# Decode attention with a gated MLP on one core: V as the moving operand of PV, in groups of four pairs, and output rows split over two PSUM rows

## The chip, the cores and the metric

The kernel runs on one core of one Trainium2 chip. Times are device microseconds of one execution. Before the change three runs took 196.67 to 197.09 us, with a median of 196.91.

The core's engines work from separate instruction streams and meet through semaphores: TensorE (PE: matrix multiply into PSUM; its weight loads, PEld, overlap its matmuls), VectorE (DVE), ScalarE (ACT), GpSimd (POOL) and SyncE (SP), which here issues the large transfers. All transfers run on the same 16 DMA engines.

## The reference

One token x (512 values) goes through two branches, and a gate mixes them. The attention branch has 32 heads, each with its own keys and values in a cache of 4096 positions of 128 values:

```python
g = sigmoid((x * gate_w).sum(-1, keepdims=True))
q = (x @ wq)                              # 32 heads x 128
scores = einsum("bhqd,bhkd->bhqk", q, k) * (128 ** -0.5)
p = softmax(scores)
o = einsum("bhqk,bhkd->bhqd", p, v)
a = o.reshape(1, 1, 4096) @ wo            # 512 outputs
h = x @ w1 + b1                           # 1376
b = where(h > 0, h, 0) ** 2 @ w2 + b2     # 512 outputs
return g * a + (1 - g) * b
```

Caches, weights and the output are bf16. K and V are 33.6 MB each, wq and wo 4.2 MB each, w1 and w2 1.4 MB each. Every byte is used once.

## The kernel before

The program is written out by hand: each engine has a list of operations in program order, and `Program` turns the dependencies between operations into semaphore waits. An engine that waits holds up everything behind it in its own list.

**Pairs.** The heads are taken two at a time, in NP = 16 pairs. The keys of a pair are one transfer of 2 MB into a slot of `Kt`: partitions 0 to 63 hold the first head of the pair and 64 to 127 the second, and each partition holds NB = 64 positions of 128 values. V lies in `Vt` in the same way. `Kt` has NK = 4 slots and `Vt` NV = 4.

**Start.** SP issues wq (line 155), then K and V. ScalarE issues five small loads: x, gate_w, b1 in two parts, b2 (lines 156 to 160). VectorE spreads x over 128 columns (`xb`, line 176). TensorE computes q, one head of each pair on each half of the partitions, into `qps` (line 185): for each chunk of four pairs four matmuls of 512 columns into PSUM rows 0 to 63, then four into rows 64 to 127. ScalarE copies the chunks to `qb` (line 189). The gate follows (lines 194 to 203).

**The loop over pairs** (lines 258 to 272). `load_k(p + 1)` and `load_v(p)` put the transfers on SP's queue. `load_k` waits for the last product that reads the slot, `load_v` for the PV that reads it (`pvs.get(p - NV)`). Then, for each half of the pair's positions:

- `product` (line 218, VectorE): K times q, element by element, 128 x 4096.
- `pe_sum` (line 232, TensorE): eight matmuls of 512 columns with the identity, which add eight pieces of the 128 products of each position and leave 16 partial sums in `red`.
- `dve_sum` (line 239, VectorE): adds the 16; that gives the scores S. It is written one half later than its product.

After both halves `exp` (line 246, ScalarE) writes E. E has two columns per position block, one for each head, with zeros at the other head's partitions. Its accumulated sums, RS, give the denominators. `pv` (line 253, TensorE) multiplies: for each of the 64 blocks of positions V is the stationary operand (128 x 128) and the two columns of E are the moving one; the 64 results add up in two columns of `o_ps`. `pv(p - 1)` stands on TensorE between `pe_sum(p, 0)` and `pe_sum(p, 1)`.

**The end.** Behind V15, SP has w1, wo in two halves (into `wbig`, the place of wq), the 96 odd rows of w2 (`w2_r`), and the other 1280 rows of w2 in two pieces (lines 277 to 289). TensorE sums the denominators over partitions (`den`), VectorE divides and applies the gate (`onorm`), and two small products bring o into columns (`op_sb`). Then TensorE does the hidden layer h (line 322), and VectorE its bias, square and gate. `to_out` (line 313) projects: for each j one row of wo (or w2) per partition, 512 outputs, is taken in four strided slices of 128 as the stationary operand, with one moving column, and everything adds up in `out_ps` (128 x 4). It goes over 32 rows of wo, the odd rows of w2, and 10 rows of w2. VectorE adds the gated b2 (line 344), and SP writes the result.

[...]

Of the kernel before, what the change touches and what calls it, by code (L numbers as in the profile page):

```python
# [71 lines left out]
def bass_gated_mix__gqa_block_cached__dense_activation_squared_relu__decode_kernel(  # L72
        nc, A_x, A_k_cache, A_v_cache, A_wq, A_wo, B_x, B_w1, B_b1, B_w2, B_b2,
                     gate_w, out):
    fp32 = mybir.dt.float32
    bf16 = mybir.dt.bfloat16
    ALU = mybir.AluOpType
    ACT = mybir.ActivationFunctionType
    AX = mybir.AxisListType

    NP = 16
    NB = 64
    HB = NB // 2
    DC = 16
    DM = 512
    F = 1376
    NJ = 10
    FT = F - 128 * NJ
    SCALE = 128.0 ** -0.5
    NK, NV = 4, 4  # L90

    k_t = A_k_cache.rearrange("a h s d -> (a h s d)").rearrange("(t p f) -> t p f", p=128, f=NB * 128)
    v_t = A_v_cache.rearrange("a h s d -> (a h s d)").rearrange("(t p f) -> t p f", p=128, f=NB * 128)
# [5 lines left out]
    gw_t = gate_w.rearrange("(p t) -> p t", t=4)  # L99
    b1_t = B_b1[0:128 * NJ].rearrange("(p j) -> p j", j=NJ)  # L100
    b1_r = B_b1[128 * NJ:F].rearrange("(p o) -> p o", o=1)
    b2_t = B_b2.rearrange("(p c) -> p c", c=4)
    out_t = out.rearrange("a b n -> (a b n)").rearrange("(p c) -> p c", c=4)

    with ExitStack() as ctx:
        def sb(name, shape, dt):
            return ctx.enter_context(nc.sbuf_tensor(name, shape, dt))

        def pb(name, shape):
            return ctx.enter_context(nc.psum_tensor(name, shape, fp32))  # L110

        wbig = sb("wbig", [128, 16384], bf16)
        w1_sb = sb("w1_sb", [128, 4, F], bf16)
        w2_sb = sb("w2_sb", [128, NJ, DM], bf16)
        w2_r = sb("w2_r", [FT, DM], bf16)
        Kt = sb("Kt", [128, NK, NB * 128], bf16)
        Vt = sb("Vt", [128, NV, NB * 128], bf16)
        prod = sb("prod", [128, 2, HB * 128], bf16)
        qb = sb("qb", [128, NP, 128], bf16)
        S = sb("S", [128, 2, NB], fp32)  # L120
        E = sb("E", [128, 2, NB, 2], bf16)
        RS = sb("RS", [128, NP, 2], fp32)
        ident = sb("ident", [128, 128], bf16)
        sel = sb("sel", [32, 4, 128], bf16)
        ones = sb("ones", [128, 128], fp32)
# [1 line left out]
        gw4 = sb("gw4", [128, 4], bf16)  # L127
        xb = sb("xb", [128, 4, 128], bf16)
        b1_sb = sb("b1_sb", [128, NJ + 1], bf16)
        b2_sb = sb("b2_sb", [128, 4], bf16)  # L130
        gate = sb("gate", [128, 4], fp32)
        rden = sb("rden", [128, 32], fp32)
        onorm = sb("onorm", [128, 32], bf16)
        ot = sb("ot", [32, 128], bf16)
        op_sb = sb("op_sb", [128, 32], bf16)
        hpre = sb("hpre", [128, NJ + 1], fp32)
        hsq = sb("hsq", [128, NJ + 1], fp32)
        hs = sb("hs", [128, NJ + 1], bf16)
        fin = sb("fin", [128, 4], bf16)

        qps = [pb(f"qps{i}", [128, 512]) for i in range(2)]
        red = [pb(f"red{i}", [128, HB, DC]) for i in range(2)]
        o_ps = pb("o_ps", [128, 32])
        h_ps = pb("h_ps", [128, NJ + 1])
        out_ps = pb("out_ps", [128, 4])
        misc = pb("misc", [128, 512])
        z_ps = misc[:, 0:1]
        den_ps = misc[:, 32:64]
# [3 lines left out]
        P = Program(nc, ctx)  # L152
# [7 lines left out]
        d_b2 = P.dma("act", "b2", lambda e: e.dma_start(b2_sb[:, :], b2_t))  # L160
# [4 lines left out]
            out=ident[:, :], in_=ident[:, :], compare_op=ALU.not_equal, fill=1.0, base=0,  # L165
            pattern=[[-1, 128]], channel_multiplier=1), i0)
        s0 = P.add("pool", lambda e: e.memset(sel[:, :, :], 0.0))
        s1 = P.add("pool", lambda e: e.affine_select(
            out=sel[:, :, :], in_=sel[:, :, :], compare_op=ALU.not_equal, fill=1.0, base=0,
            pattern=[[1, 4], [-1, 128]], channel_multiplier=4), s0)  # L170
        c_e = P.add("dve", lambda e: e.memset(E[:, :, :, :], 0.0))
        c_rs = P.add("dve", lambda e: e.memset(RS[:, :, :], 0.0))
        c_one = P.add("dve", lambda e: e.memset(ones[:, :], 1.0))
# [5 lines left out]
        q_done = []  # L179
        z_mm = None  # L180
        for c in range(4):
            last = None
            for half in range(2):
                for t in range(4):
                    last = P.add("pe", lambda e, c=c, half=half, t=t: e.matmul(  # L185
                        qps[c % 2][64 * half:64 * half + 64, :], xb[:, t, 0:64],
                        wq_v[:, t, 4 * c:4 * c + 4, half, :], start=(t == 0), stop=(t == 3)),
                        c_xb, d_wq, q_done[c - 2] if c >= 2 else None)
# [5 lines left out]
        for t in range(4):  # L194
# [5 lines left out]
        g2 = P.add("dve", lambda e: e.reciprocal(gate[:, 2:3], gate[:, 1:2]), g1)  # L200
        g3 = P.add("dve", lambda e: e.tensor_tensor(
            gate[:, 3:4], gate[:, 0:1], gate[:, 2:3], ALU.mult), g2)
        g_ap, omg_ap = gate[:, 2:3], gate[:, 3:4]


        d_k, d_v, prods, sums, exps, pvs = [], [], {}, {}, {}, {}
# [30 lines left out]
        def dve_sum(p, half):  # L237
            i = 2 * p + half
            sums[i] = P.add("dve", lambda e: e.tensor_reduce(  # L239
                S[:, p % 2, half * HB:(half + 1) * HB], red[i % 2][:, :, :], AX.X, ALU.add),  # L240
                pe_sums[i], exps.get(p - 2))

        def exp(p):
            for hh in range(2):
                q = slice(64 * hh, 64 * hh + 64)
                exps[p] = P.add("act", lambda e, q=q, hh=hh: e.activation(  # L246
                    E[q, p % 2, :, hh], S[q, p % 2, :], ACT.Exp, scale=SCALE,
                    accum_out=RS[q, p, hh:hh + 1]),
                    sums[2 * p + 1], pvs.get(p - 2), c_e, c_rs)

        def pv(p):
            for b in range(NB):
                pvs[p] = P.add("pe", lambda e, b=b: e.matmul(  # L253
                    o_ps[:, 2 * p:2 * p + 2], Vt[:, p % NV, b * 128:(b + 1) * 128],
                    E[:, p % 2, b, :], start=(b == 0), stop=(b == NB - 1)),
                    exps[p], d_v[p])

        steps = [(p, half) for p in range(NP) for half in range(2)]
        load_k(0)
        for p in range(NP):  # L260
            if p + 1 < NP:
                load_k(p + 1)
            load_v(p)
            for half in range(2):
                product(p, half)
                pe_sum(p, half)
                i = 2 * p + half
                if i >= 1:
                    dve_sum(*steps[i - 1])
                    if half == 0:  # L270
                        exp(p - 1)
                        pv(p - 1)
        dve_sum(NP - 1, 1)
        exp(NP - 1)


        d_w1 = P.dma("sp", "w1", lambda e: e.dma_start(  # L277
            w1_sb[:, :, :].rearrange("p t n -> p (t n)"), w1_t))
        d_wo = []
        for n in range(2):  # L280
            cut = slice(n * 8192, n * 8192 + 8192)
            d_wo.append(P.dma("sp", f"wo{n}", lambda e, cut=cut: e.dma_start(  # L282
                wbig[:, cut], wo_t[:, cut]), q_done[3]))
        d_w2r = P.dma("sp", "w2r", lambda e: e.dma_start(w2_r[:, :], B_w2[128 * NJ:F, :]))  # L284
        d_w2 = []
        for n, (lo, hi) in enumerate(((0, 8), (8, NJ))):
            d_w2.append(P.dma("sp", f"w2{n}", lambda e, lo=lo, hi=hi: e.dma_start(
                w2_sb[:, lo:hi, :].rearrange("p j n -> p (j n)"),
                w2_t[:, lo * DM:hi * DM])))

        pv(NP - 1)


        den = P.add("pe", lambda e: e.matmul(  # L294
# [1 line left out]
            exps[NP - 1], c_one)  # L296
        rd = P.add("dve", lambda e: e.reciprocal(rden[:, :], den_ps), den)  # L297
        on = P.add("dve", lambda e: e.scalar_tensor_tensor(
            onorm[:, :], o_ps[:, :], g_ap, rden[:, :], ALU.mult, ALU.mult), rd, pvs[NP - 1], g3)
        t0 = P.add("pe", lambda e: e.matmul(ot_ps, onorm[:, :], ident[:, :], start=True, stop=True),  # L300
                   on)
        t1 = P.add("dve", lambda e: e.tensor_copy(ot[:, :], ot_ps), t0)
# [1 line left out]
        for dq in range(4):  # L304
            sm = P.add("pe", lambda e, dq=dq: e.matmul(
                op_ps, sel[:, dq, :], ot[:, 32 * dq:32 * dq + 32], start=(dq == 0),
                stop=(dq == 3)), t1, s1)
        t2 = P.add("dve", lambda e: e.tensor_copy(op_sb[:, :], op_ps), sm)

        def to_out(w, v, first, last, *deps):  # L310
            done = None
            for c in range(4):
                done = P.add("pe", lambda e, c=c: e.matmul(  # L313
                    out_ps[:, c:c + 1], w[:, c::4], v, start=first and c == 0,
                    stop=last and c == 3, skip_group_check=True), *deps)
            return done


# [1 line left out]
        for j in range(NJ):  # L320
            for t in range(4):
                hm = P.add("pe", lambda e, j=j, t=t: e.matmul(  # L322
                    h_ps[:, j:j + 1], w1_sb[:, t, j:j + 127 * NJ + 1:NJ], x4[:, t:t + 1],
                    start=(t == 0), stop=(t == 3)), d_w1, d_x)
        for t in range(4):
            hm = P.add("pe", lambda e, t=t: e.matmul(  # L326
                h_ps[0:FT, NJ:NJ + 1], w1_sb[:, t, 128 * NJ:F], x4[:, t:t + 1],
                start=(t == 0), stop=(t == 3)), d_w1, d_x)
        h_ready = []
        for q, cols, dep in ((slice(0, 128), slice(0, NJ), d_b1), (slice(0, FT), slice(NJ, NJ + 1), d_b1r)):  # L330
            a = P.add("dve", lambda e, q=q, cols=cols: e.tensor_tensor(  # L331
                hpre[q, cols], h_ps[q, cols], b1_sb[q, cols], ALU.add), hm, dep)
            b = P.add("dve", lambda e, q=q, cols=cols: e.scalar_tensor_tensor(
                hsq[q, cols], hpre[q, cols], 0.0, hpre[q, cols], ALU.max, ALU.mult), a)
            h_ready.append(P.add("dve", lambda e, q=q, cols=cols: e.tensor_scalar(
                hs[q, cols], hsq[q, cols], gate[q, 3:4], None, ALU.mult), b, g3))
        wo_v = wbig[:, :].rearrange("p (j n) -> p j n", n=DM)
        for j in range(32):
            to_out(wo_v[:, j, :], op_sb[:, j:j + 1], j == 0, False, t2, d_wo[j // 16])
        to_out(w2_r[:, :], hs[0:FT, NJ:NJ + 1], False, False, h_ready[1], d_w2r)  # L340
        for j in range(NJ):
            done = to_out(w2_sb[:, j, :], hs[:, j:j + 1], False, j == NJ - 1, h_ready[0],
                          d_w2[0 if j < 8 else 1])
        f = P.add("dve", lambda e: e.scalar_tensor_tensor(  # L344
            fin[:, :], b2_sb[:, :], omg_ap, out_ps[:, :], ALU.mult, ALU.add), done, d_b2, g3)
        d_out = P.dma("sp", "out", lambda e: e.dma_start(out_t, fin[:, :]), f)
        P.add("sp", lambda e: e.nop(), d_out)

        P.emit()
# [28 lines left out]
```

The softmax here doesn't subtract the row's maximum and nothing guards it: scores larger than these inputs give would overflow.

## Time and profile before

| | us |
|---|---|
| median of three runs | 196.91 |
| the profiled execution | 197.14 |
| its span in the profile | 195.4 |
| TensorE matmuls busy | 125.8 |
| VectorE busy | 95.4 |
| ScalarE busy | 14.8 |
| bytes moved | 78.54 MB, mean 402 GB/s |

The page divides the span into 40 slices of 4.9 us each, with the busy share of each engine, the granted TensorE clock and the share of the DMA engines in tenths. The chain follows the last instruction back to what released it, step by step. A group row shows one source line on one engine: its form, count, busy time and mean, and the idle time ahead of it with what ended it. The timeline gives the start, the length and the count of neighbouring instructions of one kind; a bracket gives the idle time before, and its releaser. The matmul groups by line:

| line | what | count | busy us |
|---|---|---|---|
| 232 | `red`, 128 x 512 | 256 | 84.8 |
| 253 | PV, 128 x 2 | 1024 | 28.6 |
| 185 | q, 64 x 512 | 32 | 6.5 |
| 313 | projections, 128 x 1 | 172 | 6.4 |
| 322, 326 | hidden layer, 128 x 1 | 44 | 3.0 |

### The profile page before, as it was taken

The page shows a single profiled execution, that of the slowest core. Times are in us where ns is not written, and L with a number is a line of the kernel's source. Part 1 is how long each engine was busy: PE and PEld are TensorE (multiplying, and loading weights), DVE is VectorE, ACT ScalarE, POOL GpSimd, SP SyncE. Part 2 cuts the span into 40 slices and gives each one's busy share as a digit, 9 for nine tenths or more (in the row PEclk, how much of TensorE's full clock was granted, in tenths as well). Part 3 has the DMA queues.
Part 4 walks back from the last instruction along what each step waited for, and adds up shares of the span by engine and source line. Part 5 has one row for each costly group of instructions (what it writes and reads, how often), then busy time and mean ns, then how long its engine had stood idle before and what let it go on. Part 6 is the DMA issues. An engine that isn't in the chain of part 4 may idle for free.

```text
span 195.4 us, 3363 instructions
## 1 busy us (share of the span) xinstructions
PE 125.8 (64%) x1539; PEld 67.2 (34%) x1539; DVE 95.4 (49%) x82; ACT 14.8 (8%) x70; POOL 1.8 (1%) x8
## 2 busy tenths in 40 slices
PE   0019399773939396858497829393939683967552
PEld 0004135241516152415152415151515150547552
DVE  0000669917374747373747474747474744712200
ACT  2002201101010101010101010101010100110000
POOL 3000000000000000000000000000000000000000
PEclk9999859998887958888557988879795887696555
DMA  6999999999999999999999999999999999999940
GB/s 215 430 399 396 426 430 419 426 429 429 429 423 423 423 423 426 429 426 426 423 429 429 426 426 426 423 429 429 429 426 429 426 429 426 430 420 428 382 185 0
DMA packets 6430, 78.54 MB, mean 402 GB/s; under 512 B 1456, under 2 KB 1552, under 8 KB 1680
## 3 DMA queue, kind: packets, MB, share of 16 engines
q1 hardware_dynamic: 5728, 78.32, 95.3%
q8 instruction: 12, 0.20, 0.4%
q10 hardware_dynamic: 688, 0.01, 0.2%
q14 instruction: 2, 0.02, 0.0%
HBM read 78.32 MB, written 0.00 MB: 401 GB/s over the span
## 4 chain that ended last, share of the span: by engine, by line
DMA 78%; DVE 7%; PE 7%; SPq 3%; issue 3%; ACT 0%
DMA Kt<-in_A_k_cache_dram 49%; DMA w_sb<-in_B_w_dram 22%; DMA x<-in_A_x_dram 7%; DVE prod L218 6%; PE qps L185 3%; SPq L284 2%; PE red L232 2%; PE o_ps L253 1%; PE out_ps L313 1%; DVE S L239 1%; SPq L282 0%; ACT qb L189 0%; DVE xb L176 0%; SPq L277 0%; SPq L213 0%
## 5 line engine op out<-in xcount | busy, mean ns | idle before, releaser
L232 PE MATMUL red<-prod,ident 128*128 128x512 bf16 x256 | 84.8, 492 | 39.8 <-DVE prod L218 39.8
L218 DVE TENSOR_TENSOR prod<-Kt,qb 128x4096 bf16<-128x4096 bf16 x32 | 73.1, 2286 | 50.2 <-DMA Kt<-in_A_k_cache_dram 50.2
L232 PEld LDWEIGHTS red<-prod,ident 128*128 128x128 bf16 x256 | 27.5, 117 | 86.4 <-DVE prod L218 49.4
L253 PEld LDWEIGHTS o_ps<-E,Vt 128*128 128x128 bf16 x1024 | 28.6, 98 | 14.3 <-issue 11.9
L253 PE MATMUL o_ps<-E,Vt 128*128 128x2 bf16 x1024 | 28.6, 164 | 6.4 <-DMA Vt<-in_A_v_cache_dram 4.9
L239 DVE TENSOR_REDUCE S<-red 128x32 f32<-128x512 f32 x32 | 22.0, 687 | 9.9 <-PE red L232 9.9
L246 ACT ACTIVATE E<-S 64x64 bf16<-64x64 f32 x32 | 8.8, 275 | 142.2 <-DVE S L239 142.1
L185 PE MATMUL qps<-wbig,xb 128*64 128x512 bf16 x32 | 6.5, 593 | 14.0 <-DVE xb L176 14.0
L185 PEld LDWEIGHTS qps<-wbig,xb 128*64 128x64 bf16 x32 | 2.8, 162 | 17.3 <-DVE xb L176 14.0
L313 PE MATMUL out_ps<-op_sb,wbig 128*128 128x1 bf16 x128 | 4.6, 172 | 4.2 <-DMA wbig<-in_A_wo_dram 3.1
L176 DVE COPY xb<-x 128x512 bf16<-128x512 bf16 x1 | 0.4, 427 | 12.4 <-DMA x<-in_A_x_dram 12.4
L246 ACT ACTIVATION_READ_ACCUMULATOR E<-S 64x1 f32 x32 | 5.9, 185 | 0.0
L313 PEld LDWEIGHTS out_ps<-op_sb,wbig 128*128 128x128 bf16 x128 | 4.4, 118 | 4.3 <-DMA wbig<-in_A_wo_dram 3.2
L344 DVE SCALAR_TENSOR_TENSOR fin<-b_sb,gate,out_ps 128x4 bf16<-128x4 bf16 x1 | 0.2, 219 | 9.4 <-PE out_ps L313 9.4
L198 DVE TENSOR_SCALAR gate<-gate 128x1 f32<-128x1 f32 x1 | 0.2, 153 | 7.3 <-ACT gate L197 7.3
L189 ACT ACTIVATE qb<-qps 128x512 bf16<-128x512 f32 x4 | 2.4, 597 | 14.0 <-PE qps L185 14.0
L322 PE MATMUL h_ps<-x,w_sb 128*128 128x1 bf16 x40 | 2.5, 198 | 0.0
L322 PEld LDWEIGHTS h_ps<-x,w_sb 128*128 128x128 bf16 x40 | 2.4, 156 | 0.0
L297 DVE RECIPROCAL rden<-misc 128x32 f32<-128x32 f32 x1 | 0.4, 358 | 2.8 <-PE misc L294 2.8
L313 PE MATMUL out_ps<-hs,w_sb 128*128 128x1 bf16 x40 | 1.5, 172 | 0.2 <-DMA w_sb<-in_B_w_dram 0.2
L331 DVE TENSOR_TENSOR hpre<-h_ps,b_sb 128x10 f32<-128x10 f32 (+1 forms) x2 | 0.3, 158 | 2.6 <-PE h_ps L326 2.6
L189 ACT ACT_TABLE_LOAD x1 | 1.3, 1283 | 3.5 <-issue 3.5
(32 smaller groups left out, 9.2 us busy)
## 6 DMA issues: line engine op xcount, KB each, us to landing
Kt<-in_A_k_cache_dram SPq DMA_DIRECT2D x16, 2048.0 KB, 34.0
Vt<-in_A_v_cache_dram SPq DMA_DIRECT2D x16, 2048.0 KB, 36.8
wbig<-in_A_wq_dram SPq DMA_DIRECT2D x1, 4096.0 KB, 12.6
wbig<-in_A_wo_dram SPq DMA_DIRECT2D x2, 2048.0 KB, 43.0
w_sb<-in_B_w_dram SPq DMA_DIRECT2D x1, 1376.0 KB, 36.1
w_sb<-in_B_w_dram SPq DMA_DIRECT2D x1, 1024.0 KB, 43.3
w_sb<-in_B_w_dram SPq DMA_DIRECT2D x1, 256.0 KB, 39.7
w_r<-in_B_w_dram SPq DMA_DIRECT2D x1, 96.0 KB, 45.3
```

What stands on the lines that cost most here:

```text
L176: c_xb = P.add("dve", lambda e: e.tensor_copy(xb[:, :, :], x4[:, :].unsqueeze(2).to_broadcast([128, 4, 128])), d_x)
L185: last = P.add("pe", lambda e, c=c, half=half, t=t: e.matmul(qps[c % 2][64 * half:64 * half + 64, :], xb[:, t, 0:64], wq_v[:, t, 4 * c:4 * ...
L189: q_done.append(P.add("act", lambda e, c=c: e.activation(qb[:, 4 * c:4 * c + 4, :], qps[c % 2][:, :].rearrange("p (g d) -> p g d", d=128), ...
L218: prods[p, half] = P.add("dve", lambda e: e.tensor_tensor(prod[:, i % 2, :].rearrange("p (b d) -> p b d", d=128), Kt[:, p % NK, half * HB ...
L232: pe_sums[i] = P.add("pe", lambda e, c=c: e.matmul(red[i % 2][:, :, :], ident[:, :], v[:, c, :, :], start=(c == 0), stop=(c == n - 1)), pr ...
L239: sums[i] = P.add("dve", lambda e: e.tensor_reduce(S[:, p % 2, half * HB:(half + 1) * HB], red[i % 2][:, :, :], AX.X, ALU.add), pe_sums[i] ...
L246: exps[p] = P.add("act", lambda e, q=q, hh=hh: e.activation(E[q, p % 2, :, hh], S[q, p % 2, :], ACT.Exp, scale=SCALE, accum_out=RS[q, p, h ...
L253: pvs[p] = P.add("pe", lambda e, b=b: e.matmul(o_ps[:, 2 * p:2 * p + 2], Vt[:, p % NV, b * 128:(b + 1) * 128], E[:, p % 2, b, :], start=(b ...
L284: d_w2r = P.dma("sp", "w2r", lambda e: e.dma_start(w2_r[:, :], B_w2[128 * NJ:F, :]))
L297: rd = P.add("dve", lambda e: e.reciprocal(rden[:, :], den_ps), den)
L313: done = P.add("pe", lambda e, c=c: e.matmul(out_ps[:, c:c + 1], w[:, c::4], v, start=first and c == 0, stop=last and c == 3, skip_group_c ...
L322: hm = P.add("pe", lambda e, j=j, t=t: e.matmul(h_ps[:, j:j + 1], w1_sb[:, t, j:j + 127 * NJ + 1:NJ], x4[:, t:t + 1], start=(t == 0), stop ...
```

## The change

**PV.** Four positions of each partition make one matmul: V is the moving operand, 512 columns (four positions of 128 values), and the stationary operand is a block of 32 columns of E, so that a pair takes 16 matmuls in place of 64. Four neighbouring matmuls write four different groups of 32 PSUM rows of one bank. The banks are the two `qps`, which are free once q is done. Four pairs (PG = 4) share one bank: pair k of the group uses columns 8k to 8k + 7 of the 32, the others are zero in E, and all 64 matmuls of a group accumulate. At the end of a group ScalarE copies the bank to `acc_sb`. Of each row of the bank only one of the four blocks of 128 columns is the wanted one; `gather` picks and adds these with four fp32 matmuls against constants `pick`, into eight columns of `o_ps`. The gather of a group stands on TensorE after the second `pe_sum` of the pair behind the group; that of the last group directly behind its PV.

E grows to 4 KB per partition, `acc_sb` takes 2 KB, and `Vt` gets three slots in place of four.

**Projections.** In `to_out` the activations (one column) become the stationary operand and half a row of the weights (256 columns) the moving one. The two halves of the 512 outputs go to PSUM rows 0 and 64. So b2 is now needed as a row: it is loaded as one row, multiplied by the gate on VectorE ahead of the first product, and put into `out_ps` by two matmuls, which open the accumulation. The final operation is a copy of `out_ps`, and the output is written from two rows of 256.

**w2** comes in three pieces of 6, 3 and 1 rows per partition, in place of 8 and 2.

```diff
+    W2_CUTS = ((0, 6), (6, 9), (9, 10))
-    NK, NV = 4, 4
+    NK, NV = 4, 3
+    PG = 4
-    b2_t = B_b2.rearrange("(p c) -> p c", c=4)
-    out_t = out.rearrange("a b n -> (a b n)").rearrange("(p c) -> p c", c=4)
+    b2_t = B_b2.rearrange("(o n) -> o n", o=1)
+    out_t = out.rearrange("a b n -> (a b n)").rearrange("(p c) -> p c", p=2)
...
+        picks = []
+        p0 = P.add("pool", lambda e: e.memset(pick[:, :, :], 0.0))
+        for c in range(4):
+            picks.append(P.add("pool", lambda e, c=c: e.affine_select(
+                out=pick[32 * c:32 * c + 32, :, :], in_=pick[32 * c:32 * c + 32, :, :],
+                compare_op=ALU.not_equal, fill=1.0, base=0,
+                pattern=[[-2, 4], [-8, PG], [-1, 2]], channel_multiplier=1), p0))
...
+        b2m = P.add("dve", lambda e: e.tensor_scalar(
+            b2_g[:, :], b2_sb[:, :], gate[0:1, 3:4], None, ALU.mult), d_b2, g3)
+        for hh in range(2):
+            P.add("pe", lambda e, hh=hh: e.matmul(
+                out_ps[64 * hh:64 * hh + 64, :], ones[0:1, 0:64],
+                b2_g[0:1, 256 * hh:256 * hh + 256], start=True, stop=False,
+                skip_group_check=True), b2m, c_one)
...
         def exp(p):
+            k = p % PG
             for hh in range(2):
                 q = slice(64 * hh, 64 * hh + 64)
                 exps[p] = P.add("act", lambda e, q=q, hh=hh: e.activation(
-                    E[q, p % 2, :, hh], S[q, p % 2, :], ACT.Exp, scale=SCALE,
+                    E[q, k, :, 8 * k + hh:8 * k + hh + 7:2],
+                    S[q, p % 2, :].rearrange("p (g b) -> p g b", b=4), ACT.Exp, scale=SCALE,
                     accum_out=RS[q, p, hh:hh + 1]),
-                    sums[2 * p + 1], pvs.get(p - 2), c_e, c_rs)
+                    sums[2 * p + 1], pvs.get(p - PG), c_e, c_rs)
 
         def pv(p):
-            for b in range(NB):
-                pvs[p] = P.add("pe", lambda e, b=b: e.matmul(
-                    o_ps[:, 2 * p:2 * p + 2], Vt[:, p % NV, b * 128:(b + 1) * 128],
-                    E[:, p % 2, b, :], start=(b == 0), stop=(b == NB - 1)),
-                    exps[p], d_v[p])
+            k, acc = p % PG, qps[p // PG % 2]
+            for g in range(NB // 4):
+                c = g % 4
+                pvs[p] = P.add("pe", lambda e, g=g, c=c: e.matmul(
+                    acc[32 * c:32 * c + 32, :], E[:, k, g, :],
+                    Vt[:, p % NV, g * 512:(g + 1) * 512],
+                    start=(k == 0 and g < 4), stop=(k == PG - 1 and g >= NB // 4 - 4)),
+                    exps[p], d_v[p], q_done[3], copies.get(p // PG - 2))
+            if k == PG - 1:
+                G = p // PG
+                copies[G] = P.add("act", lambda e: e.activation(acc_sb[:, :], acc[:, :], ACT.Copy),
+                                  pvs[p], picked.get(G - 1))
+
+        def gather(G):
+            for b in range(4):
+                picked[G] = P.add("pe", lambda e, b=b: e.matmul(
+                    o_ps[:, 2 * PG * G:2 * PG * (G + 1)], acc_sb[:, 128 * b:128 * b + 128],
+                    pick[:, b, :], start=(b == 0), stop=(b == 3)), copies[G], *picks)
...
                     if half == 0:
                         exp(p - 1)
                         pv(p - 1)
+                    elif p and p % PG == 0:
+                        gather(p // PG - 1)
...
-        for n, (lo, hi) in enumerate(((0, 8), (8, NJ))):
+        for n, (lo, hi) in enumerate(W2_CUTS):
...
         pv(NP - 1)
+        gather(NP // PG - 1)
...
-            for c in range(4):
-                done = P.add("pe", lambda e, c=c: e.matmul(
-                    out_ps[:, c:c + 1], w[:, c::4], v, start=first and c == 0,
-                    stop=last and c == 3, skip_group_check=True), *deps)
+            for hh in range(2):
+                done = P.add("pe", lambda e, hh=hh: e.matmul(
+                    out_ps[64 * hh:64 * hh + 1, :], v, w[:, 256 * hh:256 * hh + 256],
+                    start=False, stop=last, skip_group_check=True), *deps)
...
-        f = P.add("dve", lambda e: e.scalar_tensor_tensor(
-            fin[:, :], b2_sb[:, :], omg_ap, out_ps[:, :], ALU.mult, ALU.add), done, d_b2, g3)
-        d_out = P.dma("sp", "out", lambda e: e.dma_start(out_t, fin[:, :]), f)
+        f = P.add("dve", lambda e: e.tensor_copy(fin[:, :], out_ps[:, :]), done)
+        d_out = P.dma("sp", "out", lambda e: e.dma_start(out_t, fin[0:128:64, :]), f)
```

## The prediction

> **What bounds the kernel now.** I read the page's slices, queue table and chain first, then the timeline of the two ends.
>
> ```profile
> DMA  6999999999999999999999999999999999999940
> ...
> q1 hardware_dynamic: 5728, 78.32, 95.3%
> q8 instruction: 12, 0.20, 0.4%
> ...
> DMA 78%; DVE 7%; PE 7%; SPq 3%; issue 3%; ACT 0%
> ```
>
> One queue, q1, carries all caches and weights and its 16 engines are full from the second slice to slice 38. The change moves the same bytes. So only three things can alter the time: a hole in that stream, the moment at which its slowest engine ends, and what follows its last pieces. The chain in order of time and the timeline show the last part:
>
> ```profile
> 146.74 43.30 DMA w_sb<-in_B_w_dram
> 190.04 0.05 issue
> 190.08 1.50 PE out_ps L313 x40
> 191.58 0.02 issue
> 191.60 0.22 DVE fin L344
> ```
>
> ```profile
> 182.11 2.27 PE L313 MATMUL out_ps<-op_sb,wbig 128*128 128x1 bf16 x64 [1.04 <-DVE hsq L333]
> ...
> 187.49 2.29 PE L313 MATMUL out_ps<-op_sb,wbig 128*128 128x1 bf16 x64 [3.11 <-DMA wbig<-in_A_wo_dram]
> ...
> 191.85 0.35 SPq L346 DMA_DIRECT2D out_dram<-fin  x1
> ```
>
> TensorE waits 3.11 us for the second half of wo (landed 187.44), then works 4.09 us without a real pause (187.49 to 191.58): 16 rows of wo, the odd rows of w2, ten rows of w2. Then VectorE 0.22 us, then the output transfer: issued 191.85, signals of its 16 engines from 193.1 to 194.97, span end 195.4 (0.43 later).
>
> **Does the stream stay full?** Three edits could make a hole.
>
> (a) `b2m` stands on VectorE ahead of the first product and needs b2, the last of five small loads on ScalarE's queue. Each took 4 to 6 us, as each of its eight packets per engine waits for a large packet of q1 (613 ns): b1r landed at 28.3 us, b2 at 33.3. b2 becomes a single row; I expect it one packet after b1r, at 28.9 (bounds 28.3 and 33.3). The first product started at 21.74; now it starts after `b2m` (0.5 to 0.6 us; the copy of 128x512 took 0.43) at about 29.5, 7.7 us late, TensorE behind it. Queued behind the VectorE wait are all products, and behind product (0,1) the issue of K4 on SP: 26.25 becomes 34. But SP had by then issued wq, K0 to K3 and V0 to V2, which land until 49.9. K4 still has some 12 us to spare, 7 us in the worst case. VectorE needs 2 x 2.29 + 2 x 0.69 = 6.0 us a pair, the stream brings a pair in 9.8, so the lag is gone by pair 4.
>
> (b) NV=3: V(p+3) waits for pv(p) in place of pv(p-1), and K(p+5) is queued behind it on SP. V3, free before (26.62), now waits for pv(0), by my count at 43; what lies ahead of it, K4, lands at 54.8: 9 us to spare. Later pv(p) ends 2 to 4 us after V(p) lands, with K(p+2), V(p+1), K(p+3), V(p+2), K(p+4) still queued: five transfers of 4.9 us, about 20 us of cover. The median time from issue to landing will fall from 34 to about 25 us and cost nothing. w1, wo and w2, queued behind V15 on SP, go out at about 150 in place of 141, some 17 us before the stream reaches them.
>
> (c) PV itself. It goes from 64 matmuls of 2 columns to 16 of 512, four neighbours in four column groups.
>
> ```profile
> L253 PE MATMUL o_ps<-E,Vt 128*128 128x2 bf16 x1024 | 28.6, 164 | 6.4 <-DMA Vt<-in_A_v_cache_dram 4.9
> ```
>
> That is 28.6/16 = 1.8 us a pair. For the new form the nearest row is the q projection, 512 columns in two 64-wide column groups, against `red`, 512 columns on the full array; both from the timeline's weight loads, one per matmul:
>
> ```profile
> 14.48 0.19 PEld L185 LDWEIGHTS qps<-wbig,xb 128*64 128x64 bf16 x2 [0.24 <-issue]
> 14.91 0.19 PEld L185 LDWEIGHTS qps<-wbig,xb 128*64 128x64 bf16 x2 [0.24 <-issue]
> ...
> 24.91 0.15 PEld L232 LDWEIGHTS red<-prod,ident 128*128 128x128 bf16 x1 [0.28 <-issue]
> 25.34 0.15 PEld L232 LDWEIGHTS red<-prod,ident 128*128 128x128 bf16 x1 [0.28 <-issue]
> ```
>
> `red` at clock 0.5 makes one matmul per 0.43 us, the projection two: tiles in two column groups ran side by side at full rate. (The clock records begin only at 19.81; the pairs come every 0.43 us before and every 0.21 after it, so the earlier ones were at half clock.) By this row PV costs 4 x 0.43 = 1.7 us at half clock, 0.85 at full. [...] I take 1.1 to 2.2. [...] The ScalarE copies (0.60 by the 128x512 row of L189) and gathers of the first three groups lie in idle time; so do the `pick` constants on POOL and the larger memset of E, which end long before xb at 13.6.
>
> **Where the stream ends.** In the trace each transfer has 16 signals, one per engine. Up to 33 us they lie within 0.6 us. Each instruction fetch (q8) puts one engine back by 1.3 to 1.5 us for good: after the fetch at 36.2 the last engine is 1.9 behind; eight fetches fall on different engines; the ninth and tenth (161.4, 174.2) hit the first two again, and the spread becomes 3.4. Every landing behind 161 is 1.4 us later for it, V15, wo and w2 among them. Twelve fetches of 256 instructions are TensorE's 2 x 1539. After the change it has some 720 matmul records (fp32 ones count twice, as L294 shows), 1440 instructions: five or six fetches, no engine hit twice, spread about 2. So the second half of wo lands at 185.95 in place of 187.44, **-1.5 us**; the last piece of w2 at 189.3 in place of 190.67. Bounds: 0 and -1.9.
>
> **TensorE before wo.** From pv(15) on: PV 1.1 to 2.2 (before 1.76); new are the copy (0.60 and 0.1 of signals) and four fp32 gathers at about 0.3 each by L294 (0.39 with its end): +2.0. The path to h is +1.4 to 2.4, and pv(15) starts 1.3 earlier with K15 and V15. So h ends near 181.9 (before 181.07), and the first half of wo, 32 matmuls in 16 pairs of 256 columns, takes 16 x 0.213 = 3.4 us at half clock: done near 185.3, just under the landing at 185.95. Cover gone: each further us before that point is a us at the end.
>
> **TensorE behind wo's second half.** A row of 512 outputs cost 4 x 35.5 = 142 ns as weight load plus one column (2.27/64). It now costs two tiles of 256 columns, side by side: 0.213 at half clock, 0.107 at full. The clock was 0.50 from 176.8 to the end. At half: 27 rows x 0.213 = 5.76 us against 4.09. [...] I take 5.1: **+1.0**. TensorE ends at 191.05, behind the last w2 piece (189.3 plus a last row), so the new cuts of w2 win little.
>
> **The end.** The copy of 256 columns: 0.28 for 128 and 0.19 for 32 columns (L302, L308) give 0.9 ns a column, 0.40 in all: **+0.18**. The b2 term has left it. The output goes from 128 rows of 8 bytes to 2 of 512: the first signal came 1.25 us after issue, the last at 3.12; bounds are these two, I take 1.7, near the lower since there are no longer eight tiny writes per engine: **-1.4**.
>
> Sum: -1.5 + 1.0 + 0.18 - 1.4 = -1.7. Span 193.7. With the 1.7 us around it the profiled execution's 197.1 becomes 195.4; it lay 0.2 above the median of the runs, so **195.2 us**.
>
> **The rivals.** (1) Forecast, chance 0.67: 193.8 to 196.4 from the bounds above. (2) The fetches don't come off the slowest engine, or the output transfer stays at 3.1 us: one gain of 1.5 is missing, 196.7; for it, that these are effects of single engines; chance 0.15. (3) Slower: the one-column tiles of `to_out` don't overlap, or PV's four don't. Against it, the rows of L185; for it, that four streams at once and one-column tiles stand in no row. Then 86 matmuls of 256 columns run singly: from 182.1, 24 at half clock (5 us), 62 at 0.107: 193.7; with a serial PV (3.4 to 6.8) and late wo about 196 to 197, plus 2.6 for the end: near 201 us. It decides once TensorE's work behind wo's second landing passes 6.8 us. Chance 0.12. (4) The late start and three V buffers do starve the queue: a DMA slice below 9 at 45 to 60 us; each us of hole is one of time, 199 for 4 us; chance 0.06.
>
> Under 0.2% (0.4 us) this kernel's runs can't tell a change from none. Faster: 0.67 and a third of (2), 0.72; same 0.09; slower 0.19.
>
> **What would show it.** Right: DMA slices of 9 throughout, q8 at 5 or 6, first product near 29.5, K issue to landing near 25 us, PV at 1 to 2 us a pair, TensorE ending near 191 and the output transfer under 2 us. Wrong: any wait of SP for `o_ps` or `qps` behind an empty queue, wo rows at over 0.25 us, or wo's second half still landing past 187.

## The result

The changed kernel took 194.13 us in the median of four runs (193.56 to 194.87), against 196.83 for the kernel before in the same session. The ratio is 0.9864, 95% interval 0.9819 to 0.9908. In a second series it was 193.79 (six runs) against 196.40: 0.9868, 0.9842 to 0.9894. So the change brings 2.6 to 2.7 us.

The page of the profiled execution (193.56 us) shows the same full transfer slices as before, with 5 instruction packets on q8 where there were 12. Each of them moved 16384 bytes in both traces, and is called a fetch here:

```profile
span 191.8 us, 1729 instructions
...
DMA  6999999999999999999999999999999999999991
...
q1 hardware_dynamic: 5732, 78.32, 97.0%
q8 instruction: 5, 0.08, 0.2%
```

The end of the chain, in order of time (start, length, what), now goes through the middle piece of w2, three rows per partition, which landed at 188.67. The last piece, a single row, landed at 188.98, while TensorE was still working on the middle one (its last two matmuls start at 189.04):

```profile
153.35 35.32 DMA w_sb<-in_B_w_dram
188.67 0.04 issue
188.71 0.62 PE out_ps L354 x8
189.33 0.02 issue
189.36 0.42 DVE fin L385
```

The timeline of the same end (start, length, engine and line, shape, count, idle time before):

```profile
180.95 3.35 PE L354 MATMUL out_ps<-wbig,op_sb 128*1 128x256 bf16 x32
...
185.63 1.91 PE L354 MATMUL out_ps<-wbig,op_sb 128*1 128x256 bf16 x32 [1.33 <-DMA wbig<-in_A_wo_dram]
...
187.77 1.55 PE L354 MATMUL out_ps<-w_sb,hs 128*1 128x256 bf16 x20
188.71 0.40 PEld L354 LDWEIGHTS out_ps<-w_sb,hs 128*1 128x1 bf16 x8 [0.42 <-DMA w_sb<-in_B_w_dram]
...
189.81 0.61 SPq L386 DMA_DIRECT2D out_dram<-fin  x1
```

The same 32 matmuls take 3.35 us the first time and 1.91 the second: the granted clock rose from 0.5 to 1.0 in between, at 183.94, which the prediction did not expect. The span shrank by 3.6 us against the 195.4 before. From front to back:

| | before | after | gain, us |
|---|---|---|---|
| second half of wo landed | 187.44 | 185.59 | 1.85 |
| from there to TensorE's last matmul | 4.12 | 3.72 | 0.40 |
| to the output's issue (copy and signals) | 0.29 | 0.50 | -0.21 |
| issue to the output's last signal | 3.12 | 1.57 | 1.55 |

(The output's last signals are at 194.97 and 191.38. These landings, the fetches' times and the clock's changes below are read from the records of the traces.) The profile was one of the quicker executions, so the median gains less. What differs between executions is found below.

### The profile page after: what moved, and what is told of

It is laid out like the page before. It is cut to its first block, busy times and chain, and to the rows that moved or that the text cites. A ratio compares the mean times of both kernels' runs of the same rounds, so it can differ in the third digit from the quotient of the medians.

```text
span 191.8 us, 1729 instructions
## 1 busy us (share of the span) xinstructions
PE 114.5 (60%) x721; PEld 45.6 (24%) x721; DVE 96.5 (50%) x83; ACT 17.3 (9%) x74; POOL 3.1 (2%) x13
## 4 chain that ended last, share of the span: by engine, by line
DMA 77%; DVE 10%; PE 8%; SPq 2%; ACTq 1%; issue 1%
DMA Vt<-in_A_v_cache_dram 28%; DMA w_sb<-in_B_w_dram 18%; DMA Kt<-in_A_k_cache_dram 17%; DMA b_sb<-in_B_b_dram 13%; DVE prod L238 8%; PE red L252 5%; PE qps L279 3%; DVE S L259 2%; SPq L324 1%; SPq L322 0%; ACTq L164 0%; SPq L233 0%; PE out_ps L354 0%; DVE b_g L217 0%; ACTq L162 0%
## 5 line engine op out<-in xcount | busy, mean ns | idle before, releaser
L252 PE MATMUL red<-prod,ident 128*128 128x512 bf16 x256 | 74.1, 442 | 42.6 <-DVE prod L238 42.6
L252 PEld LDWEIGHTS red<-prod,ident 128*128 128x128 bf16 x256 | 25.2, 108 | 88.6 <-DVE prod L238 50.9
L279 PE MATMUL qps<-Vt,E 128*32 128x512 bf16 x256 | 22.0, 476 | 4.7 <-DMA Vt<-in_A_v_cache_dram 3.1
L197 PE MATMUL qps<-wbig,xb 128*64 128x512 bf16 x32 | 5.0, 480 | 14.0 <-DVE xb L188 14.0
L279 PEld LDWEIGHTS qps<-Vt,E 128*32 128x32 bf16 x256 | 6.4, 109 | 20.6 <-issue 16.7
L354 PE MATMUL out_ps<-wbig,op_sb 128*1 128x256 bf16 x64 | 5.3, 335 | 1.3 <-DMA wbig<-in_A_wo_dram 1.3
L291 PEld LDWEIGHTS o_ps<-pick,acc_sb 128*128 128x128 f32 x32 | 4.1, 191 | 1.6 <-ACT acc_sb L286 1.2
L291 PE MATMUL o_ps<-pick,acc_sb 128*128 128x8 f32 x32 | 3.9, 249 | 0.7 <-ACT acc_sb L286 0.7
L354 PEld LDWEIGHTS out_ps<-wbig,op_sb 128*1 128x1 bf16 x64 | 3.1, 101 | 3.2 <-DMA wbig<-in_A_wo_dram 1.6
L286 ACT ACTIVATE acc_sb<-qps 128x512 f32<-128x512 f32 x4 | 2.4, 597 | 10.2 <-PE qps L279 10.2
## 6 DMA issues: line engine op xcount, KB each, us to landing
Kt<-in_A_k_cache_dram SPq DMA_DIRECT2D x16, 2048.0 KB, 31.6
Vt<-in_A_v_cache_dram SPq DMA_DIRECT2D x16, 2048.0 KB, 27.3
```

Of the source, the lines that this page charges most:

```text
L197: last = P.add("pe", lambda e, c=c, half=half, t=t: e.matmul(qps[c % 2][64 * half:64 * half + 64, :], xb[:, t, 0:64], wq_v[:, t, 4 * c:4 * ...
L252: pe_sums[i] = P.add("pe", lambda e, c=c: e.matmul(red[i % 2][:, :, :], ident[:, :], v[:, c, :, :], start=(c == 0), stop=(c == n - 1)), pr ...
L279: pvs[p] = P.add("pe", lambda e, g=g, c=c: e.matmul(acc[32 * c:32 * c + 32, :], E[:, k, g, :], Vt[:, p % NV, g * 512:(g + 1) * 512], start ...
L286: copies[G] = P.add("act", lambda e: e.activation(acc_sb[:, :], acc[:, :], ACT.Copy), pvs[p], picked.get(G - 1))
L291: picked[G] = P.add("pe", lambda e, b=b: e.matmul(o_ps[:, 2 * PG * G:2 * PG * (G + 1)], acc_sb[:, 128 * b:128 * b + 128], pick[:, b, :], s ...
L354: done = P.add("pe", lambda e, hh=hh: e.matmul(out_ps[64 * hh:64 * hh + 1, :], v, w[:, 256 * hh:256 * hh + 256], start=False, stop=last, s ...
```

## The experiments

All times are medians; "before" is the kernel before on the same chip in the same session (196.4 to 196.8). A spread is the time between the first and the last of the 16 signals of a transfer, one per engine.

### The changed kernel again

No edit.

> The changed kernel once more. Theory T (the working of the prediction): span 191.8 to 193.2, output transfer 1.6 us, wo's second half landed near 185.6. How long TensorE takes behind it depends on where the clock's intervals fall: 3.7 us if the clock has risen before 185.6, up to 5.8 us if not; so the runs should fall into two heaps about 1.1 us apart, and a profile of the later heap should show a clock of 0.5 behind 185. Rival C (the two heaps are a matter of the transfers): the later heap shows wo's second half landing a microsecond later, and the same TensorE time behind it.

193.79 us, six runs: 193.18, 193.41, 193.46, then 194.12, 194.52, 194.68. The profile fell into the quicker heap: span 191.5, clock up at 183.8, wo's second half landed at 185.36, output 1.6 us. For the later heap another profile served, that of the kernel with the late b2, at 194.52, whose end is the same code. The windows view (stretch, length, busy time and count of TensorE and its weight loads, then the others, granted clock, DMA share, GB/s), first of the changed kernel (the profile of 193.56 us):

```profile
181.00:184.00 3.00, 3.00 (x31) 1.78 (x32) 0.99 (x6) 0.00 (x0) 0.00 (x0) 0.51 0.99 379
184.00:187.00 3.00, 1.67 (x32) 1.11 (x30) 0.00 (x0) 0.00 (x0) 0.00 (x0) 1.00 0.96 350
187.00:190.00 3.00, 2.07 (x32) 0.98 (x28) 0.42 (x1) 0.00 (x0) 0.00 (x0) 1.00 0.18 68
```

and of the kernel with the late b2:

```profile
181.00:184.00 3.00, 2.39 (x24) 1.19 (x18) 0.00 (x0) 0.00 (x0) 0.00 (x0) 0.50 0.99 358
184.00:187.00 3.00, 1.71 (x18) 1.06 (x20) 0.00 (x0) 0.00 (x0) 0.00 (x0) 0.50 0.88 321
187.00:190.00 3.00, 3.00 (x40) 1.93 (x36) 0.00 (x0) 0.00 (x0) 0.00 (x0) 0.70 0.13 48
```

Look at the clock, the third figure from the end: 1.00 from 184 on in the one, 0.50 until 188.8 in the other. The second kernel's wo landed even earlier (185.25), but it needed 4.85 us behind it instead of 3.72 and ended 0.8 us later. Rival C falls: the transfers are not what separates these two. What ran ahead of each rise can be read from the two traces. The clock changes at 177.11, 183.94 and 190.76 in the first and at 175.15, 188.80 and 192.21 in the second; the steps between are 3.41 us or whole multiples of it, and so are all others in the first trace and in that of the kernel before. Counted from these changes in stretches of 3.41 us, the first half of wo took up 2.99 us of the stretch from 180.53 to 183.94 in the first trace, and the clock rose at its end. In the second the first half took up 2.17 us of one stretch and 1.41 of the next, and the clock stayed at 0.50; it rose at 188.80, at the end of the stretch from 185.39 that the second half filled. These are two cases, and what decides on a rise is not shown. The two halves in the second trace:

```profile
179.81 3.58 PE L355 MATMUL out_ps<-wbig,op_sb 128*1 128x256 bf16 x32 [0.41 <-DVE hsq L375]
185.29 3.58 PE L355 MATMUL out_ps<-wbig,op_sb 128*1 128x256 bf16 x32 [1.91 <-DMA wbig<-in_A_wo_dram]
```

No profile of the changed kernel itself fell into the later heap. That the clock separates its heaps in general rests on these two profiles, and on the last experiment.

### PV cut short in the kernel before

```diff
-            for b in range(NB):
+            for b in range(NB // 4):
...
-                    E[:, p % 2, b, :], start=(b == 0), stop=(b == NB - 1)),
+                    E[:, p % 2, b, :], start=(b == 0), stop=(b == NB // 4 - 1)),
```

> The kernel before with the PV sum over 16 of the 64 blocks of each pair; the other 48 are left out. 1536 TensorE instructions fewer, nothing else. Theory F (each instruction fetch puts one DMA engine back): 6 fetches in place of 12, last engine of each transfer at most 2.1 us behind the first in place of 3.4, wo's second half landed at 185.9 in place of 187.4, time 1.4 us shorter. Rival N (fetches cost nothing, TensorE's PV is hidden): the same landings within 0.3 us and the same time.

195.11 us (0.9927, 0.9908 to 0.9946): 1.3 us shorter. Its queue row, then that of the next experiment's kernel, with the padding:

```profile
q8 instruction: 6, 0.10, 0.2%
```

```profile
q8 instruction: 11, 0.18, 0.4%
```

The spread at V15 fell from 3.45 to 2.23, and wo's second half landed at 185.54 in place of 187.44. Behind the landing TensorE needed 4.31 us (4.12 before) and the output 2.91 (3.12). Theory F gave 185.9 and 1.4 us. Nothing in this kernel but the shorter PV differs, and TensorE waited for wo all the same, so it is not the shorter time on TensorE that made it faster. What is left is that fewer instructions are fetched, or that less of V is read; the next experiment decides between them.

### The changed kernel padded with instructions

```diff
+            if p < NP - 1:
+                for n in range(51):
+                    P.add("pe", lambda e: e.matmul(
+                        h_ps[:, 0:2], ident[:, :], E[:, k, 0, 0:2], start=True, stop=True), i1)
```

> The changed kernel with 51 two-column matmuls, whose result nothing uses, behind PV of each pair but the last: 765 matmuls, 1530 TensorE instructions, about 1.3 us a pair in TensorE's idle time. Theory F: q8 shows 11 fetches, the spread of the last transfers goes back to 3.4 us, the last piece of w2 lands at 190.4, time 1.4 us longer than the changed kernel. Rival N: landings and time as in the changed kernel.

194.92 us (0.9915, 0.9893 to 0.9937): 1.1 us longer than the changed kernel in the same session (1.4 was expected; the intervals just touch). Spread at V15 3.38, wo at 186.70, last piece of w2 at 190.13. The padding reads nothing of V, so it is the instructions. Rival N falls from both sides. Over all kernels, the later experiments included, by number of fetches and spread at V15:

| kernel | fetches | spread, us | wo's second half landed |
|---|---|---|---|
| before | 12 | 3.45 | 187.44 |
| padded | 11 | 3.38 | 186.70 |
| projections alone | 11 | 3.17 | 186.48 |
| PV cut short | 6 | 2.23 | 185.54 |
| both halves in one column group | 6 | 2.31 | 185.48 |
| four PSUM rows | 6 | 2.25 | 185.77 |
| PV alone | 6 | 2.12 | 185.47 |
| two V slots | 5 | 2.46 | 186.34 |
| PV in one column group | 5 | 2.21 | 185.60 |
| changed, again | 5 | 2.02 | 185.36 |
| b2 later | 5 | 1.92 | 185.25 |
| changed | 5 | 1.72 | 185.59 |

### b2 later

```diff
-        b2m = P.add("dve", ...
+            if p == 5:
+                b2m = P.add("dve", ...
```

> The changed kernel with the multiplication of b2 by the gate and its two matmuls moved from before the first product to the second half of pair 5. Theory T: the first product starts at 20.4 in place of 29.3, K4 goes out 9 us earlier, and nothing else changes: time the same within 0.3 us, as the stream had at least 10 us of cover. Rival S (the late start costs something later): 1 us or more faster.

194.53 us (0.9898, 0.9869 to 0.9927), not faster than the changed kernel in its session (193.79; the intervals overlap). It was not within the expected 0.3 us either: three of its four runs (194.52 to 195.29) lie at or above the later heap, and the profiled one of these had the late clock shown above. Whether moving b2 makes the late clock more frequent is open. The timelines' lines for the first product and the issue of K4, in the changed kernel:

```profile
29.29 4.47 DVE L238 TENSOR_TENSOR prod<-Kt,qb 128x4096 bf16<-128x4096 bf16 x2
...
33.79 0.33 SPq L229 DMA_DIRECT2D Kt<-in_A_k_cache_dram  x1
```

and here:

```profile
20.89 4.49 DVE L231 TENSOR_TENSOR prod<-Kt,qb 128x4096 bf16<-128x4096 bf16 x2
...
25.40 0.33 SPq L222 DMA_DIRECT2D Kt<-in_A_k_cache_dram  x1
```

VectorE starts 8.4 us earlier and gains nothing: wo's first half lands at 179.67 against 180.06 in the changed kernel's second profile, its second half at 185.25 against 185.36. Rival S falls.

### Both halves of a row in one column group

```diff
-                    out_ps[64 * hh:64 * hh + 1, :], v, w[:, 256 * hh:256 * hh + 256],
+                    out_ps[0:1, 256 * hh:256 * hh + 256], v, w[:, 256 * hh:256 * hh + 256],
```

(`fin` is one row of 512, the output one row.)

> The changed kernel with both halves of the projection in one PSUM row (columns 0 to 255 and 256 to 511 of row 0), so both matmuls of a weight row use the same column group; the copy is of 512 columns, the output one row. Theory P (two column groups run side by side): a weight row costs 0.43 at half clock and 0.21 at full, twice as much; 86 matmuls from 181 end near 192.7 in place of 189.3, copy 0.65, so 3 to 3.5 us longer than the changed kernel, and slower than the kernel before. Rival Q (one-column tiles never overlapped): weight rows as before, at most 0.3 us longer.

195.59 us (0.9967, 0.9941 to 0.9994). The timeline:

```profile
180.23 9.74 PE L354 MATMUL out_ps<-wbig,op_sb 128*1 128x256 bf16 x64 [0.41 <-DVE hsq L374]
```

64 matmuls take 9.74 us without a pause, where the changed kernel needed 3.35 + 1.91. TensorE ends at 192.38 (expected 192.7), the copy takes 0.68. One started every 0.21 us at half clock and every 0.11 at full, where the changed kernel started two. Theory P stands and rival Q falls: in the changed kernel the one-column tiles in two column groups ran side by side. The size was missed. By the medians of two sessions the price was 1.8 us against the changed kernel's 193.8 and not 3 to 3.5, and the kernel stayed 0.8 us below the one before. In the profile TensorE is 3.1 us later than in the changed kernel's quicker heap, but the output of a single row was complete 1.12 us after its issue in place of 1.57, which the expectation left out; and this profile, with a span of 194.6, was the longest of ten executions (the others 193.4 to 194.2). The changed kernel's median lies between its heaps, so the difference of medians is smaller still.

### PV in one column group

```diff
-                    acc[32 * c:32 * c + 32, :], E[:, k, g, :],
+                    acc[0:32, :], E[:, k, g, :],
```

(`start` and `stop` likewise mark the first and last of all 64 matmuls of a group of pairs.)

> The changed kernel with all 16 PV matmuls of a pair in one column group (PSUM rows 0 to 31): the sums of the four blocks fall together, so the attention output is another one; the instructions are the same in number and size. Theory P: PV of a pair costs 3.4 us at full clock to 6.8 at half, in place of 1.05 to 1.9; the stream stays full; the last PV puts TensorE 2.4 us late at wo's first half, and the end comes 0.5 to 1.5 us later than in the changed kernel. Rival Q: PV as in the changed kernel, time the same.

195.63 us (0.9943, 0.9921 to 0.9965), 1.8 us longer than the changed kernel by the medians of two sessions (0.5 to 1.5 was expected). The last PV of the changed kernel, then the last PV and the projections here:

```profile
173.54 1.05 PE L279 MATMUL qps<-Vt,E 128*32 128x512 bf16 x16 [1.52 <-ACT E L267]
```

```profile
174.19 3.63 PE L279 MATMUL qps<-Vt,E 128*32 128x512 bf16 x16 [1.52 <-ACT E L267]
...
184.09 6.29 PE L354 MATMUL out_ps<-wbig,op_sb 128*1 128x256 bf16 x64
```

PV takes 3.63 in place of 1.05, both at full clock; TensorE comes to wo at 184.09 in place of 180.95 (3.1 us late, 2.4 expected), no longer waits for its second half, and ends at 191.59 in place of 189.31. The stream is untouched (second half of wo at 185.60). So the four column groups overlapped almost wholly (3.63/1.05, 3.5x), and without this overlap the longer path through copy and gather no longer ends before wo's second half lands.

### PV alone, and projections alone

The PV part of the diff on the kernel before; and the other part on it, with three V slots for room.

> The kernel before with the PV part of the change alone (E, gather, three V slots); projections, b2, output and the cuts of w2 as before. Theory F: the gain is that of the fetches: 6 or 7 of them, wo's second half landed near 185.6, projections behind it 4.1 us, output transfer 3.1 us, time 1.2 us shorter than the kernel before, the same as with the PV sum cut short. Rival V (PV as such was the bound): 2 us or more shorter.

> The kernel before with the other part of the change alone: projections in two rows, b2 as a row ahead of the first product, output of two rows, w2 in three pieces; PV as before, with three V slots for the room that b2 needs. Theory F: 11 or 12 fetches, spread 3.4, last piece of w2 landed near 190.4; output transfer 1.6; time 1.2 us shorter than the kernel before. Rival H (a late first product and a slower row at half clock eat it up): no shorter than the kernel before.

PV alone: 195.01 us (0.9926, 0.9912 to 0.9941), 1.36 shorter, the same as with PV merely cut short. Its end is the old one, moved forward:

```profile
185.52 2.29 PE L344 MATMUL out_ps<-op_sb,wbig 128*128 128x1 bf16 x64 [3.10 <-DMA wbig<-in_A_wo_dram]
```

The line is that of before, 2.29 us after a wait of 3.1, two microseconds earlier. Rival V falls.

Projections alone: 195.45 us (0.9946, 0.9927 to 0.9966), 0.9 shorter. Here the output took 1.57 us and TensorE 4.83 behind wo, at half clock until 190.0. Rival H falls, though 0.7 of the 1.55 us that the output gains went to the slower rows in this execution. Theory F had 1.2 us. The two parts add up to 2.3 us of the 2.6. What the cuts of w2 are worth by themselves was not measured.

### Two V slots

```diff
-    NK, NV = 4, 3
+    NK, NV = 4, 2
```

> The changed kernel with two V slots in place of three. Theory T (five queued transfers of cover with three slots): three are left, about 12 us; DMA slices stay at 9, the median time from issue to landing of V falls to about 18 us, span 191.5 to 193. Rival S: holes in the stream, several us longer.

194.59 us (two runs, 0.9888). V lands 17.5 us after its issue, as expected, and the span of 192.6 lies in the expected range, but the start shows a dent. The window from 40 to 45, in the changed kernel and then here:

```profile
40.00:45.00 5.00, 4.11 (x31) 1.63 (x31) 5.00 (x5) 0.62 (x4) 0.00 (x0) 1.00 1.00 423
```

```profile
40.00:45.00 5.00, 4.11 (x28) 1.61 (x28) 5.00 (x4) 0.69 (x4) 0.00 (x0) 1.00 0.94 367
```

The share falls to 0.94 and the rate to 367 GB/s: V2 waits for pv(0), which the late start has put at 40 us, just where the queue runs out. From K3's first signal to V2's first 5.45 us pass, where the changed kernel has 4.88. The last weights land some 0.8 us later. So cover that was ample with three slots is just used up with two, at the start.

### A row over four PSUM rows

```diff
-            for hh in range(2):
+            for hh in range(4):
                 done = P.add("pe", lambda e, hh=hh: e.matmul(
-                    out_ps[64 * hh:64 * hh + 1, :], v, w[:, 256 * hh:256 * hh + 256],
+                    out_ps[32 * hh:32 * hh + 1, :], v, w[:, 128 * hh:128 * hh + 128],
```

(b2 and the output likewise in four pieces of 128.)

> The changed kernel with the projection's 512 outputs split over four PSUM rows of 128 columns in place of two of 256. Theory T (the later heap of runs is the half clock behind wo): a weight row costs at most 0.14 us at either clock, so TensorE is done with wo about 2 us after its landing whatever the clock, and only the last w2 piece counts; copy 0.29 in place of 0.42; all runs near 193.3, the later heap gone, median 0.5 us below the changed kernel's. Rival I (one-column tiles cost a fixed time to issue, 35 ns or more each): 0.14 to 0.2 a row at full clock, no gain or a loss of a few tenths.

193.24 us, five runs between 192.94 and 193.68; 0.9818, 0.9805 to 0.9832. The later heap is gone: the changed kernel's ten runs reach to 194.87. All five lie within 0.3 us of the changed kernel's quicker heap (193.18 to 193.60). The interval lies below that of the changed kernel's second series (0.9842 to 0.9894; the kernels were measured on two chips, each against the kernel before). The timeline, at a clock of 0.50 throughout this end:

```profile
185.82 1.88 PE L354 MATMUL out_ps<-wbig,op_sb 128*1 128x128 bf16 x64 [3.52 <-DMA wbig<-in_A_wo_dram]
...
189.47 0.29 DVE L385 CAST fin<-out_ps 128x128 bf16<-128x128 f32 x1 [8.19 <-PE out_ps L354]
```

16 rows take 1.88 us at half clock, what the changed kernel needed at full (1.91). A row starts every 0.107 us, so a matmul every 27 ns, below rival I's 35. This profile had the half clock to the end and still the span of the changed kernel's quicker profile, 191.8. Theory T stands, rival I falls. By these intervals this version is faster than both kernels.

## Why the prediction was right

It gave 195.2 us (193.8 to 196.4), faster; measured 194.13. Two of its four terms, the earlier landing and the shorter output, carry the gain, in kind and nearly in size; a third, TensorE behind wo, was too dear. Point by point:

**The stream stays full**: right. b2 came at 28.86 (predicted 28.9), the first product at 29.29 (29.5), K4 was issued at 33.79 (34) and V3 at 41.12 (43). No hole followed, and moving b2 away gained nothing. That the cover was real, and finite, is what the two slots show. One sign was missed: K's time from issue to landing fell only from 34.0 to 31.6 us, not to about 25, as V's did (27.3). K is queued behind V and lands one transfer later.

**PV in four column groups**: right in kind, a little too dear. PV took 1.05 us at full clock and 1.90 at half, where the range had 1.1 and 2.2. No run shows the range's two figures; by the row of L185 they would have been 0.85 and 1.7, and against a single column group the four gave 3.63/1.05, 3.5x. At half clock the weight loads come four to each 0.43 us:

```profile
168.57 0.16 PEld L279 LDWEIGHTS qps<-Vt,E 128*32 128x32 bf16 x4 [0.27 <-issue]
169.00 0.16 PEld L279 LDWEIGHTS qps<-Vt,E 128*32 128x32 bf16 x4 [0.27 <-issue]
```

The row of L185 was nearer: side by side at full rate, two per 0.43 us there and four here. Between full-width and 32-column matmuls, for which the prediction had no row, these traces show some time lost; its cause is not separated. In the kernel before, the first PV matmul starts one ordinary step behind the last `red`, 0.22 us at full clock and 0.43 at half; in the changed kernel 0.31 and 0.56, and the next `red` again 0.31 and 0.57 behind the last PV. That is some 0.1 us a change at full clock and 0.14 at half, 0.2 to 0.3 us a pair. The weight loads show it too, first the kernel before, then the changed one into PV and out of it:

```profile
169.12 0.15 PEld L253 LDWEIGHTS o_ps<-E,Vt 128*128 128x128 bf16 x1 [0.28 <-issue]
```

```profile
168.17 0.14 PEld L279 LDWEIGHTS qps<-Vt,E 128*32 128x32 bf16 x8 [0.83 <-issue]
...
170.00 0.13 PEld L252 LDWEIGHTS red<-prod,ident 128*128 128x128 bf16 x2 [0.84 <-issue]
```

It cost nothing here, as TensorE has more room than that in a pair (its matmuls are busy for 60% of the span).

**The stream's end**: right. Five fetches, spread 1.7 to 2.0 (about 2 predicted), wo's second half at 185.59 (185.95), the last w2 piece at 188.98 (189.3). That it is the fetches was only read from steps in the signals; the shortened and the padded kernel now show it both ways.

**TensorE before wo**: done with h at 181.02 (181.9) and with wo's first half at about 184.3 (185.3), in time.

**TensorE behind wo's second half**: the step that was off. The term "+1.0" came from 5.1 us, below the 5.76 at half clock; no run shows the 5.1, and the profile shows 3.72. In the profile the clock rose to 1.0 at 183.94, while TensorE worked on the first half of wo and before the second landed. Then TensorE is quick enough to wait for w2 (its weight loads stand idle 0.42 us ahead of the middle piece) and ends 0.64 us behind that piece's landing, so how w2 is cut can count here, where the prediction held that the cuts "win little". In the profile with the late b2 the clock rose only at 188.80, and its 4.85 us come near the predicted 5.1. A fixed term stood where two profiles show two values, and it was partly luck that the median of both came within 1.1 us of the forecast.

**The copy**: 0.42 (0.40). **The output**: 1.57 from issue to last signal (1.7), with two signals in place of 16.

Rival (2), one gain missing, is what either part alone gives: 195.0 and 195.5. Rival (3) was measured one half at a time: no overlap in the projections or in PV costs 1.8 us each; both together, for which it gave 201 us, were not run. For the projections its sum ran from 182.1 to 193.7; they ran from 180.23 to 192.38, because 182.1 was not TensorE's own time. The wait ahead of 182.11 that the line before puts down to `hsq` ended with the landing of wo's first half, at 181.97; here that half landed at 180.09. Rival (4) did not occur.

## What to carry to other kernels

In a kernel bound by its transfers, count the instructions too: here 5 fetches in place of 12 went with a spread at V15 of 1.72 us in place of 3.45, and with wo's second half 1.85 us earlier. Between a long stream and the end of the kernel look at each piece separately, what lands last, what TensorE still has to do then and at which clock, and how the output leaves. Where the clock in the tail can't be relied on, make the tail's work short at half clock, here by spreading a row over four column groups (16 rows in 1.88 us at a clock of 0.50).

## What the runs showed of the hardware

At the first fetch of 16 KB the last of a transfer's 16 signals fell back by 0.9 to 1.5 us (V2 in the changed kernel's two profiles, V1 in the one before, where the spread went from 0.59 to 1.91 us, stayed between 1.87 and 2.07, and was 3.44 with the ninth fetch). The fetch's packet itself took 0.9 to 1.1 us, a packet of caches of the same size 0.61. With 5 or 6 fetches the spread at V15 was 1.7 to 2.5 us, with 11 or 12 it was 3.2 to 3.5. (The signals carry no engine's name; that the later fetches fell on other engines is read from the steps in their order.)

With a one-column stationary operand, four matmuls of 128 columns in four column groups started every 0.107 us at half clock (1.88 us for 64 with the end of the last; four PSUM rows), and pairs of 256 columns in two groups every 0.109 us at full clock (1.91 us for 16 pairs; changed kernel) and every 0.213 at half (3.58; late b2).

In the traces of the kernel before and the changed one all changes of the granted clock lie whole multiples of 3.41 us apart. In the changed kernel the clock rose at the end of a stretch of 3.41 us of which wo's first half took up 2.99; in the kernel with the late b2 it did not after 2.17 and 1.41 us, nor in the kernel before after the 2.56 us of `red` from 24.08 to 26.64. In the profile with four PSUM rows, where each half of wo took 1.88 us, it was 0.50 from 181 to 190.

An output of one row of 1024 bytes was complete 1.12 us after its issue, one of 2 rows of 512 bytes 1.57, one of 4 rows of 256 bytes 1.64, and one of 128 rows of 8 bytes 2.8 to 3.1.
